# Moving an attention kernel's transposes and softmax sums from TensorE to DMA transposes: linear-memory attention followed by a bilinear feed-forward, one core

## The chip, the cores and the metric

The kernel runs on one core of a Trainium2 chip. A core has TensorE (PE, with its weight loads PEld), VectorE (DVE), ScalarE (ACT), GpSimd (POOL) and SyncE (SP), which work side by side, each on its own queue of instructions in the order in which the program gives them. PE writes to PSUM, which has 8 banks; the other engines read PSUM and SBUF; DMA engines move data between HBM and SBUF, and within SBUF. The metric is the device time of one execution in microseconds, the median over several runs.

## The reference

For each of 8 batches and 8 heads, 576 tokens of head size 64 are attended to through 32 memory slots. phi gives softmax weights over the tokens for each slot; with them the means k_m and v_m of k and v are formed, and each token attends to the 32 means. The result, 4608 tokens of 8 x 64 = 512 values, goes through (x w_a) * (x w_b) w_out with 1536 inner columns.

```python
a = exp(phi - max);  a = a / sum over tokens
k_m = einsum('bhsm,bhsd->bhmd', a, k)
v_m = einsum('bhsm,bhsd->bhmd', a, v)
attn = softmax(q @ k_m.T / 8)          # over the 32 slots
x = attn @ v_m                         # 4608 x 512 after the heads are put side by side
out = ((x @ w_a) * (x @ w_b)) @ w_out
```

## The kernel before

All heads of a batch are handled together. 128 partitions hold 4 heads of 32 slots, so two groups g of 4 heads j make up the 8. Six things are made for a batch: the exponentials of phi (`exp_phi`, ACT); the sums of k, v and of the weights (`kv_sums`, L205, 72 matmuls into two PSUM banks pkv); the means, scaled and laid out twice over (`take_kv`, L221, DVE, tile rep); their transposes kvT (`kv_transpose`, L235, six 128x128 TensorE transposes into pT and one DVE copy); the scores (`scores`, L278, 32 matmuls of 32 rows and 288 columns into four banks pscore) and their exponentials E (`exp_scores`, L301, ACT); and the softmax: denominators by a matmul with a block of ones (`denominators`, L308, four matmuls pD, and logarithms L on ACT) and the product with exp(-L) (`normalise`, L318, ACT and POOL), which gives A. q is transposed on DVE in 32x32 blocks of pairs (`q_transpose`, L200, four a batch, tile qT).

The values are not formed at all: `fold` (L328) multiplies the transposed means of v with w_a and w_b (tiles vab, 48 matmuls a batch, copied out of the banks pva by ACT and DVE in `take_fold`), and the up matmuls pa and pb then multiply A by those. `up_half` (L591) makes 288 tokens of one 128-column block: two matmuls pa, copied out by ACT (a_sb), two matmuls pb, multiplied with a_sb by DVE into ht. The down products take two blocks of 128 tokens together, with 7 products in the place of 8 (`two_downs`, L457, banks py, pv and px, 42 matmuls of 256 columns); POOL adds up their operands h_sums (L448), four sums of 1.64 us for each pair of blocks, and the finished blocks o_sb go out on SyncE's queue (L455).

The order is written out by hand. A batch is a period of 24 steps (`half_steps`), each with the up matmuls of one 288-token half. After each step `work.advance` issues down products at an even rate (`work.plan`), and then the step's slot is run. The slots of the period of batch b prepare batch b+1, and a name with a prime is a unit of batch b+2. The strings `second` (the period of batch 2), `every` (batches 3 to 5) and `last` (batch 6) say which unit stands in which slot (L693 to L695): exp, kv, km, kvt, qt, sc, e, den, nr, v and x are the parts named above, L loads the inputs of the batch after (phi, k, v and q, on POOL's queue), and dN, unused before, issues N down products at once. `work.settle` (L567) issues the down products that are left while a third bank is held for them. Buffers of the pool `mid` and of the inputs are double.

PSUM banks are handed out in turn by `Banks`; a matmul into a bank waits until the engine that reads its old content is done. a_sb has four buffers.

Of the kernel before, what the change touches and what calls it, by code (L numbers as in the profile page):

```python
# [18 lines left out]
def kernel(  # L19
# [26 lines left out]
    mid = ctx.enter_context(tc.tile_pool(name="mid", bufs=2))  # L46
    small = ctx.enter_context(tc.tile_pool(name="small", bufs=2))
# [25 lines left out]
    phis, qs, kvs = {}, {}, {}  # L73
# [71 lines left out]
    banks = Banks()  # L145
# [7 lines left out]
    ident = consts.tile([P, P], F16, name="ident")  # L153
# [23 lines left out]

    attn = {}
    vabs = {}

    def head(g, j):

        jj = j ^ g
        return jj % 2, 2 * g + jj // 2

    def units(b):

        u = {}
        t = {}
# [10 lines left out]
        def q_transpose(hp):  # L200
            if hp == 0:
                t["qT"] = mid.tile([P, NHP, NI * D], F16, name="qT")
            nc.vector.transpose(out=t["qT"][:, hp, :].bitcast(F32), in_=qs[b][:, hp, :].bitcast(F32))  # L203

        def kv_sums():  # L205

            t["pkv"] = [banks.take([P, 3, D], F32, "pkv", hold=True) for _ in range(2)]
            for i in range(NI):
                for g in range(2):
                    for j in range(4):  # L210
                        r, hp = head(g, j)
                        nc.tensor.matmul(  # L212
                            t["pkv"][g][0][32 * j:32 * j + 32],
                            t["exp"][64 * r:64 * r + 64, hp, i, :],
                            kvs[b][64 * r:64 * r + 64, :, hp, D * i:D * (i + 1)],
                            start=(i == 0),
                            stop=(i == NI - 1),
                            tile_position=(64 * r, 32 * j),
                        )

        def take_kv():  # L221

            t["rep"] = mid.tile([P, 2, 3, P], F16, name="rep")
            t["rphi"] = small.tile([P, 2], F32, name="rphi")
            for g in range(2):
                pkv, bank = t["pkv"][g]
                nc.vector.reciprocal(out=t["rphi"][:, g:g + 1], in_=pkv[:, 2, 0:1])
                km = pkv[:, 0].rearrange("p (d e) -> p e d", e=2).unsqueeze(2).to_broadcast([P, 2, 4, 32])
                vm = pkv[:, 1].unsqueeze(1).to_broadcast([P, 2, D])
                for out, x in ((t["rep"][:, g, 0:2].rearrange("p e (z d) -> p e z d", z=4), km),  # L230
                               (t["rep"][:, g, 2].rearrange("p (z d) -> p z d", z=2), vm)):
                    nc.vector.tensor_scalar(out=out, in0=x, scalar1=t["rphi"][:, g:g + 1], scalar2=None, op0=ALU.mult)
                banks.free(bank)

        def kv_transpose():  # L235

            t["kvT"] = mid.tile([P, 6, P], F16, name="kvT")
            pT = banks.tile([P, 6, P], F16, name="pT")
            for g in range(2):
                for x in range(3):  # L240
                    nc.tensor.transpose(out=pT[:, (2 * g + x, 4 + g)[x == 2], :], in_=t["rep"][:, g, x], identity=ident)  # L241
# [36 lines left out]
        def scores(gs):  # L278
# [7 lines left out]
            for dh in range(2):  # L286
                for z in range(2):
                    for g in gs:
                        for j in range(4):
# [8 lines left out]
                                tile_position=(row, 32 * j),  # L298
                            )

        def exp_scores(g):  # L301
# [16 lines left out]
        def normalise(g, hfs=slice(0, 2)):  # L318
# [6 lines left out]
            engine = nc.vector if b < 2 else nc.gpsimd  # L325
            engine.tensor_tensor(out=attn[b][:, g, sl], in0=t["E"][:, g, sl], in1=t["R", g][:, sl], op=ALU.mult)  # L326

        def fold(lo, hi, zs):  # L328
            if b not in vabs:
                vabs[b] = [mid.tile([P, 2, d_ff], F16, name=f"vab{x}") for x in range(2)]  # L330
            if len(zs) > 1 and b > 2:
                work.settle()
            for z in zs:
                t["pva", lo, z] = [banks.take([P, 512], F32, "pva", hold=True) for _ in range(2)]
                for j in range(4):
                    for g in range(2):
                        r, hp = head(g, j)
                        nc.tensor.matmul(  # L338
                            t["pva", lo, z][g][0][32 * j:32 * j + 32, 0:hi - lo],
                            t["kvT"][64 * r:64 * r + 64, 4 + g, M * j:M * j + M],  # L340
                            w_sbs[z][64 * r:64 * r + 64, hp, lo:hi],
                            start=True,
                            stop=True,
                            tile_position=(64 * r, 32 * j),
                        )
# [7 lines left out]
        def one(f, *a):  # L353
            return lambda: f(*a)

        for z in range(2):
            u[f"exp{z}"] = one(exp_phi, z)
            u[f"ks{z}"] = one(sums, z, 0)
            u[f"kt{z}"] = one(transpose, z, 0)
            u[f"vs{z}"] = one(sums, z, 1)  # L360
            u[f"vt{z}"] = one(transpose, z, 1)
            u[f"s{z}"] = one(scores, (z,))
            u[f"e{z}"] = one(exp_scores, z)
# [15 lines left out]
        u["sc"] = one(scores, (0, 1))  # L379
        u["kv"] = one(kv_sums)  # L380
        u["km"] = one(take_kv)
        u["kvt"] = one(kv_transpose)
        u["-"] = lambda: None
        return u

# [200 lines left out]
    work = Work()  # L586
# [147 lines left out]
```

The softmax here doesn't subtract the row's maximum and nothing guards it: scores larger than these inputs give would overflow.

## Time and profile before

| | |
|---|---|
| median of 7 runs | 243.34 us (243.11 to 243.6) |
| the profiled execution | 243.38 us |
| its span, first to last instruction | 241.7 us |
| mean granted TensorE clock | 0.996 |
| busy PE / DVE / ACT / POOL | 231.3 / 167.3 / 157.2 / 159.4 us |
| up matmuls pa and pb, 768 of 288 columns | 75.9 + 74.9 us |
| kvT transposes from rep, 36 | 3.0 us |
| scores, 256 | 5.6 us |
| denominators pD, 32 | 6.7 us |
| DMA, 34.12 MB | mean 141 GB/s |

One execution is profiled on the chip. A group of instructions is listed by line, engine, operation and tile with its count, busy time and mean; since matmuls overlap, the mean of one (0.29 us for 288 columns) is longer than the distance from one start to the next (0.12 us). The first 45 us are filled by the loading of inputs and weights; then batches follow one another every 24 to 25 us from about 78 us on, and the down products of the last tokens end at 238 us. The input loads of batches 4 to 7 are issued by POOL at 72.3, 92.6, 121.9 and 151.8 us.

### The profile page before, as it was taken

What the parts mean: (1) busy time and instruction counts of PE and PEld (TensorE: products, weight loads), DVE (VectorE), ACT (ScalarE), POOL (GpSimd) and SP (SyncE); (2) the same over time, 40 slices, a digit from 0 to 9 for tenths busy, and PEclk for the clock granted to TensorE, in tenths of its full rate; (3) what the DMA queues carried; (4) which work ended last, traced back from release to release, by engine and by line L of the source; (5) the groups of instructions that cost most, each with busy time, mean ns of one, the idle gap of its engine ahead of it and who ended that gap; (6) DMA issues with size and microseconds to landing.
All of it is one profiled execution on the core that took longest, in us unless ns stands there. A gap on an engine that the chain in (4) does not pass through costs nothing.

```text
span 241.7 us, 7803 instructions
## 1 busy us (share of the span) xinstructions
PE 231.3 (96%) x3110; PEld 170.0 (70%) x3110; DVE 167.3 (69%) x406; ACT 157.2 (65%) x410; POOL 159.4 (66%) x135
## 2 busy tenths in 40 slices
PE   7868999999999999999999999999999999999993
PEld 7544664446757867777788777777787778888882
DVE  4736784469858869976984759865986586756652
ACT  2266671569697599598756777587856777465430
POOL 7953244599979549973989759882939087946001
PEclk9999999999999999999999999999999999999998
DMA  6999999999958934992279542794220303032154
GB/s 235 234 197 207 206 258 205 255 208 285 219 130 187 223 75 93 248 185 46 50 171 213 138 90 61 182 207 119 49 46 17 72 17 74 11 81 65 44 127 114
DMA packets 25764, 34.12 MB, mean 141 GB/s; under 512 B 2016, under 2 KB 19808, under 8 KB 25728
## 3 DMA queue, kind: packets, MB, share of 16 engines
q0 software_dynamic: 19264, 23.14, 51.5%
q1 hardware_dynamic: 5952, 9.70, 15.9%
q10 hardware_dynamic: 512, 0.79, 1.0%
q8 instruction: 24, 0.39, 0.6%
q14 instruction: 12, 0.10, 0.1%
HBM read 42.47 MB, written 9.44 MB: 215 GB/s over the span
## 4 chain that ended last, share of the span: by engine, by line
PE 75%; DMA 16%; ACT 2%; POOL 2%; DVE 2%; issue 1%; DVEq 0%; POOLq 0%
PE pa L594 17%; PE py L466 17%; PE pb L594 16%; PE pv L466 9%; DMA wo_sb<-in_moe_w_out_dram 6%; DMA kv_sb<-in_v_dram 5%; DMA wb_sb<-in_moe_w_b_dram 5%; PE pva L338 4%; PE px L466 4%; PE pkv L212 2%; PE po L391 2%; PE pD L315 1%; PE pscore L292 1%; PE pT L241 1%; DVE ht L605 1%
## 5 line engine op out<-in xcount | busy, mean ns | idle before, releaser
L605 DVE TENSOR_TENSOR ht<-a_sb,pb 128x288 f16<-128x288 f16 x168 | 73.3, 448 | 36.3 <-ACT a_sb L602 26.9
L594 PEld LDWEIGHTS <-vab 128*128 128x128 f16 x768 | 71.6, 98 | 27.2 <-issue 9.2
L602 ACT CAST a_sb<-pa 128x288 f16<-128x288 f32 x168 | 66.9, 408 | 26.3 <-PE pa L594 24.8
L594 PE MATMUL pa<-A,vab 128*128 128x288 f16 x384 | 75.9, 287 | 0.2
L594 PE MATMUL pb<-A,vab 128*128 128x288 f16 x384 | 74.9, 286 | 1.0 <-ACT vab L350 0.5
L448 POOL TENSOR_TENSOR h_sums<-ht 128x768 f16<-128x768 f16 x28 | 45.9, 1640 | 32.5 <-DVE ht L605 32.5
L466 PEld LDWEIGHTS <-h_sums 128*128 128x128 f16 x384 | 37.3, 98 | 7.0 <-issue 0.5
L350 DVE CAST vab<-pva 128x512 f16<-128x512 f32 (+1 forms) x52 | 32.5, 644 | 4.6 <-PE pva L338 4.2
L350 ACT CAST vab<-pva 128x512 f16<-128x512 f32 (+1 forms) x52 | 28.1, 570 | 9.4 <-PE pva L338 9.3
L466 PEld LDWEIGHTS <-ht 128*128 128x128 f16 x288 | 28.1, 98 | 5.7 <-issue 0.4
L466 PE MATMUL py<-w_sums,h_sums 128*128 128x256 f16 x192 | 30.4, 272 | 0.0
L448 POOL TENSOR_TENSOR h_sums<-ht,h_sums 128x768 f16<-128x768 f16 x14 | 23.0, 1643 | 0.9
L448 POOL TENSOR_TENSOR h_sums<-h_sums,ht 128x768 f16<-128x768 f16 x14 | 22.9, 1638 | 0.9
L326 POOL TENSOR_TENSOR A<-E,R 128x576 f16<-128x576 f16 x12 | 15.3, 1276 | 7.5 <-ACT R L324 7.2
L305 ACT ACTIVATE E<-pscore 128x288 f16<-128x288 f32 x32 | 11.4, 418 | 11.9 <-PE pscore L292 11.8
L466 PE MATMUL pv<-w_sums,h_sums 128*128 128x256 f16 x96 | 16.2, 273 | 0.0
L466 PE MATMUL py<-wo_sb,ht 128*128 128x256 f16 x96 | 16.0, 273 | 0.0
L473 ACT ACTIVATE u<-py 128x256 f32<-128x256 f32 x32 | 12.5, 391 | 5.0 <-PE py L466 4.8
L466 PE MATMUL py<-w_sums,ht 128*128 128x256 f16 x96 | 15.5, 272 | 0.1
L466 PE MATMUL px<-wo_sb,ht 128*128 128x256 f16 x96 | 15.4, 273 | 0.0
L316 ACT ACTIVATE L<-pD 128x288 f32<-128x288 f32 x32 | 11.6, 427 | 5.1 <-PE pD L315 4.9
L203 DVE STREAM_TRANSPOSE qT<-q_sb 128x288 f32<-128x288 f32 x32 | 14.4, 463 | 0.1
(65 smaller groups left out, 277.6 us busy)
## 6 DMA issues: line engine op xcount, KB each, us to landing
out_dram<-o_sb SPq DMA_DIRECT2D x68, 128.0 KB, 3.0
phi_sb<-in_phi_dram POOLq DMA_DIRECT2D x8, 576.0 KB, 6.2
kv_sb<-in_v_dram POOLq DMA_DIRECT2D x7, 576.0 KB, 10.6
kv_sb<-in_k_dram POOLq DMA_DIRECT2D x7, 576.0 KB, 8.6
q_sb<-in_q_dram POOLq DMA_DIRECT2D x6, 576.0 KB, 13.5
wo_sb<-in_moe_w_out_dram POOLq DMA_DIRECT2D x6, 256.0 KB, 13.7
q_sb<-in_q_dram POOLq DMA_DIRECT2D x4, 288.0 KB, 9.7
wa_sb<-in_moe_w_a_dram POOLq DMA_DIRECT2D x2, 512.0 KB, 13.6
```

What stands on the lines that cost most here:

```text
L203: nc.vector.transpose(out=t["qT"][:, hp, :].bitcast(F32), in_=qs[b][:, hp, :].bitcast(F32))
L305: nc.scalar.activation(out=Ev[:, g, :, z, :], in_=pss, func=AF.Exp, scale=1.0 / (8.0 * CS))
L316: nc.scalar.activation(out=t["L", g][:, sl], in_=pD, func=AF.Ln)
L326: engine.tensor_tensor(out=attn[b][:, g, sl], in0=t["E"][:, g, sl], in1=t["R", g][:, sl], op=ALU.mult)
L338: nc.tensor.matmul(t["pva", lo, z][g][0][32 * j:32 * j + 32, 0:hi - lo], t["kvT"][64 * r:64 * r + 64, 4 + g, M * j:M * j + M], w_sbs[z][64 ...
L350: engine_copy(out=vabs[b][z][:, g, lo:hi], in_=pva[:, 0:hi - lo])
L448: engine.tensor_tensor(out=out, in0=in0, in1=in1, op=op)
L466: nc.tensor.matmul(po, lhs[:, i], rhs[:, i], start=first and i == 0, stop=i == KH - 1, skip_group_check=not first)
L473: nc.scalar.mul(out=x, in_=po, mul=scale)
L594: nc.tensor.matmul(ps, vabs[b][x][:, g, P * i:P * (i + 1)], attn[b][:, g, HALF * hf:HALF * (hf + 1)], start=(g == 0), stop=(g == 1))
L602: nc.scalar.copy(out=a_sbs[b, i, hf], in_=ps)
L605: nc.vector.tensor_tensor(out=ht[:, i, t0:t0 + HALF], in0=a_sbs.pop((b, i, hf)), in1=ps, op=ALU.mult)
```

## The change

For batches from `TURNED = 3` on, three things are turned by DMA transposes on SyncE's queue: q (`q_turn`, 128 x 2304), the means of k and v (`kv_turn`, four blocks of 128x128), which `take_kv` now lays out for k and v in one scaling for each group, and, for batches 4 to 7, the exponentials. The scores then contract over 64 rows in one pass instead of over 32 in two (`token_scores`). For batches 4 to 7 the exponentials E are turned so that tokens lie on partitions (`e_turn`, 128 x 1152); DVE sums the 32 slots of each head (`token_sums`), POOL and DVE multiply with the reciprocals (`token_normalise`), and a second DMA transpose turns the result back (`a_turn`). Batch 3 keeps the denominators by matmul. The slots are placed anew, with down products issued by name (dN). Batches 0 to 2 and the work before the period of batch 2 are as they were.

```diff
+    TURNED = 3
...
+        def q_turn():
+            t["qT"] = mid.tile([P, NHP, NI * D], F16, name="qT")
+            nc.sync.dma_start_transpose(out=t["qT"].rearrange("p c f -> p (c f)").rearrange("p (n x) -> p n x", x=P),
+                                        in_=qs[b].rearrange("p c f -> p (c f)"))
...
-        def take_kv():
+        def take_kv(gs=range(2)):
...
-            for g in range(2):
+            for g in gs:
                 pkv, bank = t["pkv"][g]
                 nc.vector.reciprocal(out=t["rphi"][:, g:g + 1], in_=pkv[:, 2, 0:1])
...
+                if b >= TURNED:
+                    parts = ((t["rep"][:, 2 * g:2 * g + 2].rearrange("p x (z d) -> p x z d", z=2),
+                              pkv[:, 0:2].unsqueeze(2).to_broadcast([P, 2, 2, D])),)
+                for out, x in parts:
                     nc.vector.tensor_scalar(out=out, in0=x, scalar1=t["rphi"][:, g:g + 1], scalar2=None, op0=ALU.mult)
...
+        def kv_turn():
+
+            t["kvT"] = mid.tile([P, 6, P], F16, name="kvT")
+            n = 4 if b >= TURNED else 6
+            nc.sync.dma_start_transpose(out=t["kvT"][:, 0:n], in_=t["rep"][:, 0:n].rearrange("p x d -> p (x d)"))
...
+        def token_scores():
+            t["E"] = mid.tile([P, 2, S], F16, name="E")
+            work.settle()
+            qTv = t["qT"].rearrange("p c f -> p (c f)").rearrange("p (n x) -> p n x", x=P)
+            for g in range(2):
+                t["pss", g] = [banks.take([P, 5 - y, 64], F32, "pscore", hold=True) for y in range(2)]
+            for g in range(2):
+                for x in range(2):
+                    for j in range(4):
+                        r, hp = head(g, j)
+                        y = (hp + x) % 2
+                        n = (NI * hp + y) // 2
+                        nc.tensor.matmul(
+                            t["pss", g][y][0][32 * j:32 * j + 32],
+                            t["kvT"][64 * x:64 * x + 64, 2 * g, M * j:M * j + M],
+                            qTv[64 * x:64 * x + 64, n:n + 5 - y, 64 * r:64 * r + 64],
+                            start=True,
+                            stop=True,
+                            tile_position=(64 * x, 32 * j),
+                        )
...
+        def e_turn():
+            t["ET"] = mid.tile([P, 2, S], F16, name="E").rearrange("p g s -> p (g s)").rearrange("p (n x) -> p n x", x=P)
+            nc.sync.dma_start_transpose(out=t["ET"], in_=t["E"].rearrange("p g s -> p (g s)"))
+
+        def blocks(x):
+            return t["ET"][:, slice(0, 5) if x == 0 else slice(5, 9)].rearrange("p n (j m) -> p (n j) m", m=M)
+
+        def token_sums(x):
+            if x == 0:
+                t["sum"] = small.tile([P, 36], F32, name="sum")
+            out = t["sum"][:, slice(0, 20) if x == 0 else slice(20, 36)]
+            nc.vector.tensor_reduce(out=out, in_=blocks(x), axis=mybir.AxisListType.X, op=ALU.add)
+            nc.vector.reciprocal(out=out, in_=out)
+
+        def token_normalise(x):
+            sums = t["sum"][:, slice(0, 20) if x == 0 else slice(20, 36)]
+            engine = (nc.gpsimd, nc.vector)[x]
+            engine.tensor_tensor(out=blocks(x), in0=blocks(x), in1=sums.unsqueeze(2).to_broadcast(list(blocks(x).shape)),
+                                 op=ALU.mult)
+
+        def a_turn():
+            attn[b] = mid.tile([P, 2, S], F16, name="A")
+            nc.sync.dma_start_transpose(out=attn[b].rearrange("p g s -> p (g s)").rearrange("p (n x) -> p n x", x=P),
+                                        in_=t["ET"].rearrange("p n x -> p (n x)"))
...
-    second = "v2_+x2a_+exp0 x2b_ exp1 - kv+km qt0 kvt+qt1 - qt2+qt3 sc+e0 e1+v0+x0a+x0b den0 nr0+v1+x1a - x1b+exp0' L exp1' v2+x2a den1+qt0'+qt1' x2b - qt2'+nr1+kv'+km' - - kvt'+qt3'"
-    every = "- sc+e0 e1 den0 v0+x0a+x0b - - nr0+exp0' - - v1+x1a qt0' x1b+den1 exp1' - v2+x2a+x2b nr1+qt1' kv'+km' qt2' - qt3' - kvt'+L -"
-    last = "sc+e0 - e1 - v0+x0b - x0a den1 - - den0 v1+x1b x1a+nr0 - - - - nr1+v2+x2a - - - - - x2b"
+    second = "v2_+d1+exp0+x2a_ exp1+d6+x2b_ qd+kv+km0+km1+kvd - - d4 - - sc+e0 - e1+d3+v0+d2+x0a+x0b den0 - v1+nr0+x1a x1b+qd' L+exp0'+d5 - v2+x2a exp1'+x2b - - kv'+den1+nr1+km' kvd' - d7"
+    every = "sc+e0+e1+d3+ed+d3 - - v0+x0a+x0b - sm0 sm1 - tn1+exp0' d5+tn0+exp1' ad v1+x1b+x1a+kv'+km0' qd'+km1' kvd' - - v2+x2b - - - - - L+x2a"
+    last = "sc+e0+e1+ed - - v0+x0b+d5 - - sm0+d4 tn0 sm1+d5 tn1 x0a+v1+x1a+x1b - ad - - v2+x2a - - - d4 - x2b"
```

The new units' names: qd, kvd, ed and ad are the four DMA transposes, km0 and km1 the scaling of one group, sm0 and sm1 the row sums, tn0 (POOL) and tn1 (DVE) the products. `token_exp_scores` reads the four banks pscore as `exp_scores` did, with 320 or 256 columns each.

More of the change, by code (lines that the diff above doesn't have):

```diff
@@ L219, in kv_sums @@
                         )
-        def take_kv():
-            t["rep"] = mid.tile([P, 2, 3, P], F16, name="rep")
-            t["rphi"] = small.tile([P, 2], F32, name="rphi")
-            for g in range(2):
+        def take_kv(gs=range(2)):
+            if gs[0] == 0:
+                t["rep"] = mid.tile([P, 6, P], F16, name="rep")
+                t["rphi"] = small.tile([P, 2], F32, name="rphi")
+            for g in gs:
                 pkv, bank = t["pkv"][g]
@@ L229, in take_kv @@
                 vm = pkv[:, 1].unsqueeze(1).to_broadcast([P, 2, D])
-                for out, x in ((t["rep"][:, g, 0:2].rearrange("p e (z d) -> p e z d", z=4), km),
-                               (t["rep"][:, g, 2].rearrange("p (z d) -> p z d", z=2), vm)):
+                parts = ((t["rep"][:, 2 * g:2 * g + 2].rearrange("p e (z d) -> p e z d", z=4), km),
+                         (t["rep"][:, 4 + g].rearrange("p (z d) -> p z d", z=2), vm))
+                if b >= TURNED:
+                    parts = ((t["rep"][:, 2 * g:2 * g + 2].rearrange("p x (z d) -> p x z d", z=2),
+                              pkv[:, 0:2].unsqueeze(2).to_broadcast([P, 2, 2, D])),)
+                for out, x in parts:
                     nc.vector.tensor_scalar(out=out, in0=x, scalar1=t["rphi"][:, g:g + 1], scalar2=None, op0=ALU.mult)
@@ L238, in kv_transpose @@
             pT = banks.tile([P, 6, P], F16, name="pT")
-            for g in range(2):
-                for x in range(3):
-                    nc.tensor.transpose(out=pT[:, (2 * g + x, 4 + g)[x == 2], :], in_=t["rep"][:, g, x], identity=ident)
+            for x in range(6):
+                nc.tensor.transpose(out=pT[:, x, :], in_=t["rep"][:, x], identity=ident)
             nc.vector.tensor_copy(out=t["kvT"], in_=pT)
+        def kv_turn():
+            t["kvT"] = mid.tile([P, 6, P], F16, name="kvT")
+            n = 4 if b >= TURNED else 6
+            nc.sync.dma_start_transpose(out=t["kvT"][:, 0:n], in_=t["rep"][:, 0:n].rearrange("p x d -> p (x d)"))
         def sums(g, x):
@@ L299, in scores, with token_exp_scores @@
                             )
+        def token_scores():
[18 more added lines that the diff above has]
+                        )
+        def token_exp_scores(g):
+            Ev = t["E"].rearrange("p g (i s) -> p g i s", s=64)
+            for y in range(2):
+                pss, bank = t["pss", g][y]
+                nc.scalar.activation(out=Ev[:, g, y::2, :], in_=pss, func=AF.Exp, scale=1.0 / (8.0 * CS))
+                banks.free(bank)
         def exp_scores(g):
@@ L339, in fold @@
                             t["pva", lo, z][g][0][32 * j:32 * j + 32, 0:hi - lo],
-                            t["kvT"][64 * r:64 * r + 64, 4 + g, M * j:M * j + M],
+                            t["kvT"][64 * r:64 * r + 64, 2 * g + 1 if b >= TURNED else 4 + g, M * j:M * j + M],
                             w_sbs[z][64 * r:64 * r + 64, hp, lo:hi],
@@ L362, in units @@
             u[f"s{z}"] = one(scores, (z,))
-            u[f"e{z}"] = one(exp_scores, z)
+            u[f"e{z}"] = one(token_exp_scores if b >= TURNED else exp_scores, z)
+            u[f"km{z}"] = one(take_kv, (z,))
             u[f"den{z}"] = one(denominators, z)
@@ L378, in units @@
             u[f"qt{x}"] = one(q_transpose, x)
-        u["sc"] = one(scores, (0, 1))
+        u["sc"] = token_scores if b >= TURNED else one(scores, (0, 1))
+        u["qd"] = q_turn
+        u["ed"] = e_turn
+        for x in range(2):
+            u[f"sm{x}"] = one(token_sums, x)
+            u[f"tn{x}"] = one(token_normalise, x)
+        u["ad"] = a_turn
         u["kv"] = one(kv_sums)
@@ L382, in units @@
         u["kvt"] = one(kv_transpose)
+        u["kvd"] = one(kv_turn)
         u["-"] = lambda: None
```

## The prediction

> **What bounds the kernel.** I read the page's busy times first, then the busy times by stretch, because the start, the steady part and the tail have different limits.
>
> ```profile
> PE 231.3 (96%) x3110; PEld 170.0 (70%) x3110; DVE 167.3 (69%) x406; ACT 157.2 (65%) x410; POOL 159.4 (66%) x135
> ...
> 102.00:203.00 101.00, 101.00 (x1306) 77.62 (x1285) 74.14 (x175) 74.37 (x197) 72.98 (x52) 1.00 0.51 105
> 203.00:238.00 35.00, 34.39 (x299) 28.90 (x296) 21.93 (x51) 16.61 (x44) 14.32 (x11) 1.00 0.29 64
> ```
>
> In the stretch lines the columns after the time and its length are busy PE, PEld, DVE, ACT and POOL, then PE clock, DMA share and GB/s. From 102 to 203 us TensorE is busy for 101.00 of 101 us at full clock, while no other compute engine passes 75 us. The waits of PE in that part are short "issue" gaps of its weight loads. So a microsecond of matmul taken out there is a microsecond off the end, and a microsecond for which PE waits is one on it. Between 70 and 102 us it is 31.80 of 32.
>
> Then the timeline of one batch, for what the matmuls concerned really cost. Columns: start, duration, engine, line, operation. Durations overlap in the pipeline, so I take start to start.
>
> ```profile
> 153.72 0.50 PE L241 MATMUL pT<-ident,rep 128*128 128x128 f16 x6
> ...
> 154.05 0.41 PE L594 MATMUL pa<-A,vab 128*128 128x288 f16 x2
> ...
> 156.71 0.47 PE L292 MATMUL pscore<-qT,kvT 32*32 32x288 f16 x32
> ...
> 157.11 0.42 PE L594 MATMUL pa<-A,vab 128*128 128x288 f16 x2
> ...
> 158.87 0.41 PE L315 MATMUL pD<-E,ones 128*128 128x288 f16 x2
> ...
> 159.11 0.41 PE L594 MATMUL pa<-A,vab 128*128 128x288 f16 x2
> ...
> 160.13 0.41 PE L338 MATMUL pva<-wa_sb,kvT 64*32 64x512 f16 x8
> 160.36 0.40 PE L338 MATMUL pva<-wb_sb,kvT 64*32 64x512 f16 x8
> ...
> 160.69 0.36 PEld L594 LDWEIGHTS <-vab 128*128 128x128 f16 x4 [0.42 <-issue]
> ```
>
> Six transposes 0.33 us, 32 score matmuls 0.40, two denominators 0.24, sixteen folds 0.56.
>
> Last the DMA view, in a stretch without an input load (first line) and in one where a load of a batch fills the engines (the other two).
>
> ```profile
> out_dram<-o_sb SPq DMA_DIRECT2D x6, 128.0 KB, 2.4
> ...
> DMA  0684905999899999999999999999999999999400
> ...
> out_dram<-o_sb SPq DMA_DIRECT2D x4, 128.0 KB, 6.0
> ```
>
> The same 128 KB store on SyncE's queue lands 2.4 us after its issue between 108 and 121 us, and 6.0 us after it between 122 and 137 us, while a batch's phi, k, v and q come in (that load takes some 14 us). The new transposes go on this queue.
>
> **What the Trainium skill says.** "VectorE: DVE Perf Modes", section "The three transpose paths", gives 390 ns on TensorE and 1309 ns by DMA for one 128x128 block. TensorE's six cost 0.33 us here, 55 ns each in a row, so its figures are of single ones. "Advanced Engine Details and Errata", "X-Bar Transpose (TRN2)", says such DMAs are as fast as plain ones; no run here shows one. "DMA: Bandwidth & Descriptors", "Issuing engines are not separate DMA queues", says that all issuing engines share the same 16 DMA engines: the 2.4 against 6.0 us agrees. The first page also has `tensor_reduce` at one element a cycle only ("Rules for kernel authors").
>
> **The change, part by part.**
> *PE.* Batches 3 to 7 lose six transposes each: 5 x 0.33 = 1.65 us. Batches 4 to 7 lose four denominators each: 8 pairs x 0.24 = 1.92. The 32 score matmuls of 32 rows become 16 of 64 rows with 320 or 256 columns. The nearest row is the fold (16 of 64 rows, 512 columns, 0.56): 0.56 x 288/512 = 0.31, bounds 0.20 (half of 0.40) and 0.40. Gain 5 x 0.09 = 0.45 (0 to 1.0). Sum 4.0 us. Down products and up matmuls are only moved.
> *ACT*, per turned softmax: four logarithms (0.427) and two exponentials (0.709) go, 3.1 us. *POOL*: two of 1.28 go, one of 640 columns with an fp32 operand comes (1.28 x 640/576 = 1.4, up to double). *DVE*, per batch: four transposes (0.463), one copy (0.551), four scalings (two 0.483, two 0.341) go, 4.05 us; two scalings (0.97) come, with turned softmax two row sums of 640 and 512 elements (0.75 and 0.6, from the 0.684 of a 512-column cast), two reciprocals (0.16 or a little more), one product (0.6): 3.2. All three have a quarter of their time free, so I book nothing for them.
> *DMA.* 18 transposes: q 576 KB (batches 3 to 7), kv 128 KB (the same), E and A 288 KB each (batches 4 to 7). Their cost is only what waits for them. The smallest I give a kv turn is a store's 2.4 us, E 3 to 4; in a load the store's 3.6 us extra comes on top at most, since the turn doesn't write to HBM I take half of it: kv 4.3, E 5.5.
>
> SyncE's queue is in order, but a q turn stands behind only stores, so it starts when its load has landed: for batch 3 at about 70 us, in the gap before the load of batch 4 (issued at 72.3 to 75.3). It is needed at 83. Later ones have over 8 us. Hidden. The A turns are issued some 11 us before their batch begins. Hidden. Three are not clearly hidden; I count PE work in the new order with the durations above, up matmuls at 0.12, down at 0.11.
>
> 1. *Means of batch 3.* Sums end at about 76.7, scaling takes 1.3, turn 4.3 in the load of batch 4: 82.3. PE reaches the scores at 83.5 (84.3 before, less transposes and moved work). Free; with 6 to 6.7 us it is 0.5 to 1.2 late. I book 0.3.
> 2. *Means of batch 4.* Sums are now at the end of the period of batch 2, the turn one slot before the scores. PE has 2 denominators, 12 up and 17 down matmuls between: 0.24 + 1.46 + 1.86 = 3.6 us. Needed: scaling with its place behind one product, 1.5, plus the turn, in the load of batch 5 (issued about 93): 4.3. Late by 2.2 us (0.3 with 2.4, 3.9 with 6). In it lies the second wait there: the last denominators of batch 3 moved behind these sums, and two logarithms, an exponential and POOL's product (2 x 0.43 + 0.71 + 1.28 + one copy 0.41 = 3.3) face 2.6 us of PE work before A of batch 3 is read. Queued behind: everything of PE.
> 3. *E of batches 4 to 7.* The row sums stand in DVE's queue; behind them the products ht, and for those PE's banks and ACT's four a_sb buffers. DVE arrives there 4 to 5 us after E is issued (four exponentials x 0.42, then three products, two folds' copies, two more products), and PE has about 3 us of banks after that. The loads of batches 6 and 7 are issued a few us before E of batches 5 and 6. 5.5 us is covered; I book 0.3 in all.
>
> Sum: -4.0 + 0.3 + 2.2 + 0.3 = -1.2. The profiled execution took 243.38 us, its span 241.7 and 1.7 around it; the median is 243.34, the same within 0.04. 243.34 - 1.2 = **242.1 us**.
>
> **Rivals.**
> *Slower: turns in a load take as long as stores or longer.* For it: 6.0 us in the DMA view, 5.8 to 6.7 from 74 to 90 us, at less than half of E's bytes; the cover of point 2 is short in any case. Against it: the turn writes SBUF. Priced: 1.0 at the scores of batch 3, 3.9 at those of batch 4, and E at 9 us leaves 9 - 4.5 - 3 = 1.5 for each of batches 5 and 6: 7.9 - 4.0 = +3.9, 247.2. It decides from a kv turn of 5.5 us, where point 2 costs 1.5 + 5.5 - 3.6 = 3.4 and the other two bring the sum to the 4.0 gained.
> *Slow in themselves.* 1.31 us a block in a row: E 11.8, kv 5.2, q 23.6 us. Batch 3 waits 70 + 23.6 - 83.5 = 10 us, batch 4 3.1, each E 4.3: +26, 269. Against it: the other page's "as fast as plain".
> *All hidden.* A turn lands like a free store: only 0.3 of point 2 is left, 239.6.
> *The gain is just eaten*, within 0.2%: a kv turn of about 5.3 us.
>
> **Numbers.** 0.2% (0.5 us) is about what a measurement of this kernel can tell. Likeliest, mostly hidden, 240.2 to 242.8: 0.35. All hidden, 239.2 to 240.2: 0.13. Eaten: 0.12. Late in loads, 243.9 to 249: 0.31. Slow turns, 250 to 270: 0.09. So faster 0.48, same 0.12, slower 0.40. The likeliest two have 239.2 to 242.8 for themselves. Below 239.5 lie about 0.05, above 248 some 0.14: range 239.5 to 248.
>
> **What would show it.** The rows of pT<-ident,rep and pD fall from 36 to 6 and from 32 to 16 matmuls, PE busy by 4 us. The list of DMA issues gives kv, E, A and q turns; about 4.3, 5.5, 4 and 5 us. The score rows of batches 3 and 4 show PE's waits (0.3 and 2.2 us); DVE waits for E under 2 us. Wrong would be: E over 8 us or a wait on kvT over 4 (slower), or q turns of batch 3 issued into the load; PE idle between 102 and 203 us above 1.5 us is a wait that I have not seen.

## The result and the profile after

The changed kernel takes 260.87 us (median of 12 runs, 259.71 to 264.01), the kernel before 243.37 us beside it: a ratio of 1.072, 95% interval 1.070 to 1.0743. It is 17.5 us slower. The forecast was 242.1 us, its range 239.5 to 248, its first choice "faster" (0.48, against 0.40 for slower): wrong in sign and in size. The profiled execution below was the slowest of the twelve, 264.01 us with a span of 262.3, which is why sums over it come out some 3 us above the median, and the ratios in this document leave out runs in a slower state, which the medians include, so that the two can differ a little.

The page's busy times and the row of PE's granted clock:

```profile
PE 234.8 (90%) x2984; PEld 170.0 (65%) x2984; DVE 164.7 (63%) x391; ACT 150.4 (57%) x386; POOL 154.3 (59%) x131
...
PEclk9999999999999689959999999999599999999998
```

PE has 126 matmuls fewer than before and yet 3.5 us more busy time. The clock row says why: it falls to 0.5 or 0.6 in three of the 40 slices, and a matmul at half clock is busy longer (0.66 us where it took 0.41, shown further below). Now the busy times by stretch (the columns are those of the stretch lines in the prediction: time, length, PE, PEld, DVE, ACT, POOL, clock, DMA share, GB/s).

```profile
84.00:88.00 4.00, 0.44 (x16) 0.15 (x16) 0.00 (x0) 0.00 (x0) 0.00 (x0) 0.84 1.17 219
88.00:92.00 4.00, 4.00 (x40) 1.76 (x29) 1.28 (x3) 2.53 (x7) 0.00 (x0) 0.50 0.17 55
...
102.00:203.00 101.00, 87.43 (x1111) 65.94 (x1108) 63.75 (x149) 56.78 (x147) 60.22 (x44) 0.93 0.82 151
```

From 102 to 203 us PE stands still for 13.6 of 101 us, where it never stood before. From 84 to 88 us every compute engine is all but idle while the DMA engines are full; from 88 to 92 the DMA engines are nearly free and PE works at a clock of 0.50. The list of waits names what ended each gap (total, times, longest):

```profile
PE pscore L329 <- DMA kvT<-rep: 10.3, 2, 6.1
...
DVE sum L383 <- DMA E<-E: 7.9, 2, 4.5
...
PE pa L671 <- DVE ht L682: 4.1, 1, 4.1
...
PE py L543 <- DVE o_sb L554: 3.3, 1, 3.3
```

Two waits of PE are for the transposed means themselves (batch 3: 4.2 us, batch 4: 6.1). The other two name DVE, but DVE had been waiting for E of batches 5 and 6. Together PE waits 17.7 us. Its waits name no input load, so no batch came late because its own inputs did. The chain of what ended last has the DMA transposes in it (start, time):

```profile
78.11 9.40 DMA kvT<-rep
...
105.02 8.59 DMA kvT<-rep
...
173.07 8.75 DMA E<-E
```

POOL issues the input loads of batches 4 to 7 at 72.3, 100.2, 132.7 and 164.4 us. Each of these transposes was issued 5 to 9 us after the start of one; so was E of batch 5 (issued at 140.97, 9.1 us). The DMA view of 104 to 116 us shows one transpose in a load and one just after it (the first row is the busy share of the 16 engines in 40 slices, the last number of the others the us from issue to landing):

```profile
DMA  9999999999999999999999999999999999630000
...
kvT<-rep SPq DMA_TRANSPOSE x1, 8.6
E<-E SPq DMA_TRANSPOSE x1, 3.2
```

The means (128 KB), issued at 105.0 in the load, land at 113.6, about 0.6 us before the engines fall free. E of batch 4, more than twice the bytes, is issued at 115.6 and takes 3.2 us. This pair is the case in short: the transposes are not slow in themselves; they are late beside a load.

### The profile page after: what moved, and what is told of

Same layout as the page of the kernel before. It is cut to its first block, busy times and chain, and to the rows that moved or that the text cites. A ratio compares the mean times of both kernels' runs of the same rounds, so it can differ in the third digit from the quotient of the medians.

```text
span 262.3 us, 7547 instructions
## 1 busy us (share of the span) xinstructions
PE 234.8 (90%) x2984; PEld 170.0 (65%) x2984; DVE 164.7 (63%) x391; ACT 150.4 (57%) x386; POOL 154.3 (59%) x131
## 3 DMA queue, kind: packets, MB, share of 16 engines
q1 hardware_dynamic: 29824, 15.67, 29.2%
## 4 chain that ended last, share of the span: by engine, by line
PE 75%; DMA 15%; ACT 4%; DVE 3%; issue 2%; DVEq 0%; SPq 0%; POOLq 0%
PE pa L671 17%; PE pb L671 16%; PE py L543 14%; DMA kvT<-rep 7%; PE pv L543 7%; PE pva L407 5%; PE po L468 4%; PE px L543 3%; DMA E<-E 3%; DMA phi_sb<-in_phi_dram 2%; DMA out_dram<-o_sb 2%; PE pkv L218 2%; PE pk L271 1%; PE pscore L308 1%; PE pscore L329 1%
## 5 line engine op out<-in xcount | busy, mean ns | idle before, releaser
L671 PEld LDWEIGHTS <-vab 128*128 128x128 f16 x768 | 74.0, 100 | 31.5 <-issue 11.3
L671 PE MATMUL pa<-A,vab 128*128 128x288 f16 x384 | 78.0, 293 | 4.2 <-DVE ht L682 4.1
L671 PE MATMUL pb<-A,vab 128*128 128x288 f16 x384 | 77.1, 293 | 1.0 <-ACT vab L419 0.5
L543 PEld LDWEIGHTS <-h_sums 128*128 128x128 f16 x384 | 38.0, 100 | 10.0 <-issue 2.8
L543 PE MATMUL py<-w_sums,h_sums 128*128 128x256 f16 x192 | 32.0, 282 | 0.0
L543 PE MATMUL px<-wo_sb,ht 128*128 128x256 f16 x96 | 16.1, 280 | 0.0
L550 ACT ACTIVATE u<-py 128x256 f32<-128x256 f32 x32 | 12.5, 391 | 5.1 <-PE py L543 4.8
L342 ACT ACTIVATE E<-pscore 128x320 f16<-128x320 f32 (+1 forms) x20 | 6.7, 416 | 14.0 <-PE pscore L329 14.0
L389 POOL TENSOR_TENSOR E<-E,sum 128x640 f16<-128x640 f16 x4 | 5.1, 1263 | 16.1 <-PE py L543 8.9
L543 PE MATMUL pv<-wo_sb,h_sums 128*128 128x256 f16 x96 | 14.1, 277 | 0.0
L195 ACT ACTIVATE exp_sb<-phi_sb 128x576 f16<-128x576 f32 x16 | 10.9, 696 | 5.4 <-DMA phi_sb<-in_phi_dram 5.4
## 6 DMA issues: line engine op xcount, KB each, us to landing
wa_sb<-in_moe_w_a_dram POOLq DMA_DIRECT2D x2, 512.0 KB, 13.6
```

The costliest lines, as they stand in the source:

```text
L195: nc.scalar.activation(out=t["exp"][:, 2 * z:2 * z + 2, :, :], in_=phis[b][:, 2 * z:2 * z + 2, :].rearrange("p c (i m) -> p c i m", m=M), ...
L342: nc.scalar.activation(out=Ev[:, g, y::2, :], in_=pss, func=AF.Exp, scale=1.0 / (8.0 * CS))
L543: nc.tensor.matmul(po, lhs[:, i], rhs[:, i], start=first and i == 0, stop=i == KH - 1, skip_group_check=not first)
L550: nc.scalar.mul(out=x, in_=po, mul=scale)
L671: nc.tensor.matmul(ps, vabs[b][x][:, g, P * i:P * (i + 1)], attn[b][:, g, HALF * hf:HALF * (hf + 1)], start=(g == 0), stop=(g == 1))
```

## The experiments

Three theories are put against each other in the expectations. The first (A): the transposes are quick but land late beside an input load. The second (B): the transposes, or the new order of the slots, cost time with or without loads. The third (C): part of the time is PE's clock after a long wait. The expectations are quoted as they stood before each run.

### No loads beside, in both kernels

```diff
     def load(b):
+        if b >= 4:
+            phis[b], kvs[b], qs[b] = phis[b - 2], kv_sbs[b % 2], qs[b - 2]
+            return
         load_phi(b)
```

> The kernel before, with the input loads of batches 4 to 7 left out (these batches compute on the inputs of batches 2 and 3 that are still in SBUF, so the output of half the batches differs). It is the control of the next run. Both theories: TensorE bounds it, the loads are hidden, 243.3 us, within 0.5.

> The changed kernel with the same loads left out. Theory A (the DMA transposes are quick by themselves and are held up by the input loads on the same DMA engines): kv turns land in 2.4 to 3 us, E turns in 3.2 to 4, no wait of PE over 1 us, and the time is 4.0 us less matmul work plus some 0.5 us: about 240 us. Theory B (the turns, or the new order of the units, are slow in themselves): kv and E turns still near 9 us, waits of PE at the scores of batches 3 and 4 remain, 250 us or more.

Batches 4 to 7 use the inputs of earlier batches here. The kernel before does not care: 243.45 us, ratio 1.0006 (0.9997 to 1.0016). The changed kernel falls from 260.87 to 238.63 us, ratio 0.9805 (0.9788 to 0.9822). Its DMA view:

```profile
qT<-q_sb SPq DMA_TRANSPOSE x5, 4.8
kvT<-rep SPq DMA_TRANSPOSE x5, 2.4
E<-E SPq DMA_TRANSPOSE x4, 3.2
A<-E SPq DMA_TRANSPOSE x4, 3.5
```

and its stretch line, PE full again:

```profile
102.00:203.00 101.00, 101.00 (x1227) 78.76 (x1226) 79.53 (x181) 68.90 (x179) 64.79 (x41) 1.00 0.49 93
```

The second theory falls: with free DMA engines all 18 transposes and the new order of slots gain 4.8 us against the same kernel before. All of the loss, and more, needs a load beside the transposes. That leaving out the loads also spares the waits for inputs does not matter here: PE had none in the changed kernel. This kernel's span of 237.0 us is the base of the sums below.

### Only the means of batches 3 and 4 by TensorE

```diff
             n = 4 if b >= TURNED else 6
+            if b in (3, 4):
+                pT = banks.tile([P, n, P], F16, name="pT")
+                for x in range(n):
+                    nc.tensor.transpose(out=pT[:, x, :], in_=t["rep"][:, x], identity=ident)
+                nc.vector.tensor_copy(out=t["kvT"][:, 0:n], in_=pT)
+                return
             nc.sync.dma_start_transpose(
```

with these units two slots later and one slot later in `second`.

> Only the means of batches 3 and 4 go back to TensorE transposes (two slots later than their DMA turns stood); the rest is the changed kernel. Theory A: PE's two waits for kvT (4.2 and 6.1 us in the profile) and the half clock after each (about 2.4 us each) go, four transposes of 0.055 us come for each: 260.9 - 10.3 - 4.8 + 0.4 = 246 us. If the waits merely move to the next late thing: 255 us or more.

253.79 us (249.45 to 271.08), ratio 1.0455 (1.0406 to 1.0505). Both waits for kvT are gone, but 7 us come back instead of 15. The profiled execution is the quickest of the six, 249.45 us; what the others lose beyond it no trace shows. Without the waits everything is earlier, and so E of batch 4, which in the changed kernel came after the load (3.2 us), is now issued within the load of batch 5:

```profile
102.47 7.76 DMA E<-E
...
161.58 8.30 DMA E<-E
```

```profile
PE pa L677 <- DVE ht L688: 3.7, 1, 3.7
PE pb L677 <- DVE ht L688: 3.3, 1, 3.3
...
PE py L549 <- DVE o_sb L560: 1.7, 1, 1.7
```

A wait removed moved the next transpose into a load: three waits behind E (batches 4, 5 and 6) in the place of two.

### The loads of batches 6 and 7 eight slots earlier

```diff
-    every = "sc+e0+e1+d3+ed+d3 - - v0+x0a+x0b - sm0 sm1 - tn1+exp0' d5+tn0+exp1' ad v1+x1b+x1a+kv'+km0' qd'+km1' kvd' - - v2+x2b - - - - - L+x2a"
+    every = "sc+e0+e1+d3+ed+d3 - - v0+x0a+x0b - sm0 sm1 - tn1+exp0' d5+tn0+exp1' ad v1+x1b+x1a+kv'+km0' qd'+km1' kvd' L - v2+x2b - - - - - x2a"
```

> Only the loads of batches 6 and 7 are moved, from slot 22 to slot 14 of the string every, so that they end before or about when E of the next batch is turned. Theory A: E turns of batches 5 and 6 land in under 6 us, the two waits of PE (3.3 and 4.1 us) and one half-clock stretch (2.4 us) go: 260.9 - 9.8 = 251 us. If the E turns are slow for another reason: 260 to 261 us.

255.72 us, ratio 1.0479 (1.0411 to 1.0548): 5 of the 10 us expected. POOL issued these loads only 3 to 6 us earlier (129.5 and 158.4 us): its queue is not tied to PE's slots. E still takes 6.4 and 7.2 us, not under 6. That is enough to let PE's two waits on E fall from 3.3 and 4.1 to 0.5 and 2.6 us in the profiled execution (258.62 us), since the load beside them ends earlier; the waits on kvT stay (10.6 us).

### The same 128 KB copied, not transposed

```diff
             n = 4 if b >= TURNED else 6
+            if b in (3, 4):
+                nc.sync.dma_start(out=t["kvT"][:, 0:n], in_=t["rep"][:, 0:n])
+                return
             nc.sync.dma_start_transpose(
```

> The turn of the means of batches 3 and 4 becomes a plain DMA copy of the same 128 KB (not transposed, so the values of these batches are wrong), on the same queue at the same place. Queue theory (anything put on this queue in a load waits for the load): still 6 to 9 us to landing, waits of 3 us or more at both scores, 255 to 261 us. Form theory (the transposes' 256-byte packets are what is held up): 3 to 5 us, as little as 0 to 2 us of wait, 247 to 250 us.

The chain of this kernel has both copies:

```profile
93.76 6.37 DMA kvT<-rep
...
114.86 5.60 DMA kvT<-rep
```

A plain copy within SBUF in a load takes 5.6 to 6.4 us, as long as a store does there (6.0 us), so the place of the data is not the point. The transposed form of the same bytes, issued at about the same point of its load (4.8 and 5.9 us after the load's start, the copies 4.3 and 5.9), takes 8.6 to 9.4. With free DMA engines a copy takes 2.0 us (a later run has it) and the transpose 2.4: a load adds 3.6 to 4.4 us to the one and 6.2 to 7.0 to the other, so some 2.6 us of its extra are the form's. Both theories of the expectation have a part. Median 255.62 us, ratio 1.0453 (1.0391 to 1.0516), in the range of the first of the two. PE still waits 4.3 us for the copies. (The profiled execution, 268.08 us, has a wait of 12.9 us at 49 to 62 us, before any of this, behind a single product of DVE that took 13.6 us, as one execution of the kernel of before without loads has it too (12.5 us of wait); it stays out of the sum below.)

### PE kept busy in the two waits

```diff
             work.settle()
+            if b in (3, 4):
+                fill({3: 19, 4: 28}[b])
             qTv = t["qT"].rearrange("p c f -> p (c f)")
```

> The changed kernel, with matmuls of zeros put on PE right ahead of the scores of batches 3 and 4: 19 and 28 of 512 columns, 0.21 us each at full clock, 4.1 and 6.0 us, as long as PE waited there for kvT. Theory C (an idle PE is given half the clock afterwards): the kvT waits are filled, the clock stays at 1.0 there, and what the slow stretches after them cost (two times about 2.4 us) comes back: 256 us. Theory A without C (only the wait itself costs): 261 us, no gain.

260.17 us, ratio 1.0665 (1.0629 to 1.0701): hardly less than the changed kernel. The clock did hold,

```profile
70.00:102.00 32.00, 31.29 (x452) 21.34 (x444) 21.13 (x48) 22.42 (x57) 21.26 (x19) 1.00 0.80 151
```

(and at the second fill too), but the transposes landed later still (9.92 and 10.35 us), so that 2.4 us of waiting were left behind the fills, and the waits on E, now 2.4 and 3.1 us, cost 3.2 us of clock. By its time alone the run speaks against the third theory; with several things moving at once it decided nothing, and the question of the clock was put again without loads.

### Late transposes without a load, bare and filled

```diff
             n = 4 if b >= TURNED else 6
+            if b in (3, 4):
+                for h in range(3):
+                    hop = mid.tile([P, 6, P], F16, name="rep")
+                    nc.sync.dma_start(out=hop[:, 0:n], in_=t["rep"][:, 0:n])
+                    t["rep"] = hop
             nc.sync.dma_start_transpose(
```

The loads of batches 4 to 7 are left out as above. The second of the two has the fills of the last section as well.

> The changed kernel without the input loads of batches 4 to 7 (these batches compute on older inputs), with three plain copies of the 128 KB on SyncE's queue ahead of the DMA transpose of the means of batches 3 and 4: the transposes are late without any load beside them. Copies of 2.4 us and the transpose of 2.4 us make about 10 us from the first issue, against 9.4 and 8.6 us in the loads. PE then waits about 4.8 us at the scores of batch 3 and 7.5 us at those of batch 4, 12.3 us in all. Theory 'waits alone': 238.6 + 12.3 = 250.9 us. Theory 'waits and half clock after them' (5 us at half clock after each, 2.5 us lost twice): 255.5 us, and PE's clock under 0.6 for some 5 us after both waits.

> As the kernel with the late transposes and no loads, with 19 and 28 matmuls of zeros (128x512, 0.22 us each, results not used) on PE ahead of the scores of batches 3 and 4, so that PE has work in most of the two waits (4.1 and 6.1 us of it). Theory 'half clock after waits': the clock stays at 1.00 and the time falls by some 4 us against the kernel without the fill, to about 251 us. Theory 'waits alone': the same time as without the fill, 0.3 us either way.

The bare kernel takes 251.26 us (250.56 to 251.81), ratio 1.0324 (1.0306 to 1.0343). A copy took 2.0 us and not 2.4, so the waits are shorter than expected:

```profile
PE pscore L337 <- DMA kvT<-rep: 9.3, 2, 5.9
```

238.63 + 9.3 = 247.9; 3.3 us more were measured. The stretches in which PE works after its two waits:

```profile
88.00:92.00 4.00, 4.00 (x35) 2.07 (x34) 2.34 (x5) 2.83 (x8) 0.00 (x0) 0.65 0.32 73
...
112.00:116.00 4.00, 4.00 (x36) 2.60 (x28) 1.39 (x4) 2.52 (x7) 0.00 (x0) 0.66 0.38 74
```

Summed over stretches of 1 us, PE's busy time times one minus its clock is 3.3 us in this execution: the missing 3.3 us. The filled kernel takes 250.47 us (250.37 to 250.93), with a clock of 1.00 throughout in its profiled execution: 238.63 + 10.4 of fill (19 take 4.19 us) + 1.4 of waiting = 250.4. It is 0.8 us quicker, not 4 and not the same, because fills and rest of the wait were 2.5 us longer than the waits that they replaced (3.3 - 2.5 = 0.8); that the clock holds, and that the sum closes without a clock term when it does, is what the third theory says. So these waits cost their own length and then the clock.

### The loads set apart from the transposes

The means of batches 3 and 4 by TensorE again; the q transpose of batch 4 and the load of batch 5 earlier; and in `every` the load in two parts, k and v (La) after E is expected to land, phi and q (Lb) after the transposes of q and the means:

```diff
-    second = "v2_+d1+exp0+x2a_ exp1+d6+x2b_ qd+kv+km0+km1+kvd - - d4 - - sc+e0 - e1+d3+v0+d2+x0a+x0b den0 - v1+nr0+x1a x1b+qd' L+exp0'+d5 - v2+x2a exp1'+x2b - - kv'+den1+nr1+km' kvd' - d7"
-    every = "sc+e0+e1+d3+ed+d3 - - v0+x0a+x0b - sm0 sm1 - tn1+exp0' d5+tn0+exp1' ad v1+x1b+x1a+kv'+km0' qd'+km1' kvd' - - v2+x2b - - - - - L+x2a"
+    second = "v2_+d1+exp0+x2a_ exp1+d6+x2b_ qd+kv+km0+km1 - kvd d4 - - sc+e0 qd' e1+d3+v0+d2+x0a+x0b den0 L v1+nr0+x1a x1b exp0'+d5 - v2+x2a exp1'+x2b - - kv'+den1+nr1+km' - kvd' d7"
+    every = "sc+e0+e1+d3+ed+d3 - - v0+x0a+x0b - sm0 sm1+La - tn1+exp0' d5+tn0+exp1' ad v1+x1b+x1a+kv'+km0' qd'+km1' kvd' - - v2+x2b+Lb - - - - - x2a"
```

> A version that keeps turns and loads apart: means of batches 3 and 4 by TensorE, q of batch 4 turned and batch 5 loaded some slots earlier, and the loads of batches 6 and 7 in two parts, k and v in slot 6 (when E has landed) and phi and q in slot 16 (when kv has). Theory A: no E turn over 5 us, the kernel without loads plus 0.4 us of transposes, 239 to 240.5 us, 0.985 of the kernel before. If loads and turns can't be kept apart: 243 us or more.

243.62 us (20 runs, 241.71 to 257.84), ratio 0.9969 (0.9946 to 0.9991): some 17 us of the changed kernel's loss are gone with all loads in place, but not the 239 to 240.5 us expected. One late transpose is left, E of batch 4 in the load of batch 5 (issued at 91 us):

```profile
102.40 7.46 DMA E<-E
```

```profile
PE pb L677 <- DVE ht L688: 3.0, 1, 3.0
```

Four more runs tried to free this one too.

> As the kernel with the loads set apart, but k and v of the batch after are issued by POOL behind the product that waits for E, so that they cannot start before E has landed. The transpose of E of batch 4 then shares its time with the last 4 us of the load of batch 5 only: about 4.5 us in the place of 7.46, and PE's wait of 3.0 us falls to about 0.3. Theory 'transposes late in loads': 243.6 - 2.7 = 240.9 us. Rival 'the load comes late in turn' (k and v some 5 us later, sums of the next batch wait): 243 to 246 us.

In `every`, La moved from slot 6 to slot 9, behind the product on POOL. 259.67 us, ratio 1.0627 (1.0581 to 1.0673), far outside both expectations. E of batch 4 came down to 4.8 us, but k and v, issued at 110.5 us, and phi and q at 117.8 now met the transposes of A, q and the means of batch 5, all three. The DMA view of 108 to 140 us:

```profile
A<-E SPq DMA_TRANSPOSE x1, 10.6
qT<-q_sb SPq DMA_TRANSPOSE x1, 23.2
kvT<-rep SPq DMA_TRANSPOSE x1, 13.0
```

```profile
PE pscore L335 <- DMA kvT<-rep: 15.4, 2, 12.9
```

SyncE itself was held for 10.6 us at issuing the q transpose, and the transpose of the means stood behind it. Instead of one wait of 3 us there are one of 12.9 and one of 2.6.

> As the kernel with POOL's loads behind E, and the load of batch 5 six slots earlier (issued at about 83 in the place of 91 us), so that it has ended when E of batch 4 is issued at 102. All E transposes about 3.2 to 4 us, no PE wait above 1 us from 78 us on. Theory 'transposes late in loads': 238.6 (no loads at all) plus 0.5 for what loads still do, 239.2 us. Rival: the load of batch 5 stands on that of batch 4 and delays q of batch 4 or its phi: PE waits of 2 us or more before 104 us, 242 us or more.

The same with the load of batch 5 at slot 6 of `second`: 263.26 us, ratio 1.0796 (1.0756 to 1.0837). E now takes 3.2 us, as expected, but the means of batch 5 take 17.5 us (wait 15.7), and q of batch 4 costs 2.1.

> As the kernel with the loads set apart (k and v of the later batches stay at slot 6), with the load of batch 5 three slots earlier, directly behind the q transpose of batch 4: issued at about 87 in the place of 91 us, ended at about 101.5, just ahead of E of batch 4 at 102.4. Theory 'a transpose lands when the load beside it ends': E of batch 4 takes about 4 us in the place of 7.46, PE's wait of 3.0 us goes, 243.6 - 2.7 = 240.9 us. Rival 'the q transpose of batch 4 takes its place': q, issued at 89, lands after 102 and the scores of batch 4 wait 1 to 2 us: 243 us or more.

> The same with the load of batch 5 five slots earlier, issued at about 84 us, right behind the end of the load of batch 4. E of batch 4 is free of it by 3 us: 3.2 us. The q transpose of batch 4, issued at 89 with 12 us of the load beside it, takes 12 us or more and the scores of batch 4 at 102 wait for it by up to 2 us, as in the kernel with the load at 82 us (2.1 us): 242 us. Theory without such a limit: 240.9 us as with three slots.

These two left La at slot 6 and moved only the load of batch 5, in `second` from slot 12 to slot 9 or 7. They take 242.99 us, ratio 0.9976 (0.9967 to 0.9984), and 243.48 us, ratio 1.0004 (0.9986 to 1.0022). The load went out at 81.9 and 82.8 us, not at 87 and 84: POOL takes its next instruction when its own inputs are there. The rival was right, q took E's place:

```profile
PE pscore L335 <- DMA qT<-q_sb: 2.4, 1, 2.4
PE pscore L335 <- DMA kvT<-rep: 1.6, 2, 1.2
```

With the load at slot 9 the wait on E is gone, 2.4 us are spent waiting for q and 1.6 for means. It has the lowest median with real inputs, 0.4 us below the kernel of before (243.39 beside it) and 4.4 us above the kernel without loads. By the ratios it (0.9976) and the first version (0.9969) are 0.2 to 0.3% below the kernel of before; neither is clearly the better one, and both differ from it by next to nothing.

### The sum that closes

Each profiled span against 237.0 us, the span without loads. "Clock" is PE's busy time times one minus its clock, summed over stretches of 1 us from 60 to 245 us; "work" is what the edit adds on PE (0.22 us a fill matmul; 0.4 us for eight transposes).

| kernel | this execution (median) | span | PE's waits from 60 us on | clock | work | 237.0 + sum |
|---|---|---|---|---|---|---|
| changed | 264.0 (260.9) | 262.3 | 17.7 | 7.8 | 0 | 262.5 |
| means 3, 4 by TensorE | 249.5 (253.8) | 247.8 | 8.7 | 1.5 | 0.4 | 247.6 |
| loads earlier | 258.6 (255.7) | 256.9 | 13.7 | 5.9 | 0 | 256.6 |
| waits filled | 260.2 (260.2) | 258.5 | 7.9 | 3.2 | 10.3 | 258.4 |
| late, no loads | 251.2 (251.3) | 249.4 | 9.3 | 3.3 | 0 | 249.6 |
| late, no loads, filled | 250.4 (250.5) | 248.7 | 1.4 | 0 | 10.4 | 248.8 |
| loads apart | 243.6 (243.6) | 241.9 | 3.0 | 1.7 | 0.4 | 242.1 |
| loads apart, load of 5 at slot 9 | 243.0 (243.0) | 241.3 | 4.0 | 0 | 0.4 | 241.4 |

All of these close within 0.3 us, each for its one execution. Of those not in the table, La at slot 9 and the load of batch 5 at slot 7 miss by 0.6 and 0.7 us: their executions reach the batches later (the load of batch 4 goes out at 73.0 and 73.1 us, not at 72.2). The changed kernel is thus its kernel without loads, plus four waits on late transposes, plus the clock that these waits cost.

## Why the prediction was wrong, step by step

**PE's work: right, 0.8 us too small.** The sum gave -4.0 us; with no transpose late, -4.8 were measured. The row of 16 score matmuls took 0.40 us and not 0.31, so that term (0.45 us) was nothing; what makes up the other 1.2 us was not found out. That DVE, ACT and POOL stay covered held: with free DMA engines PE is busy for 101.00 of 101 us. So did "Hidden" for the q and A transposes of the changed kernel. (DVE's row sums were put at 0.75 and 0.6 us from a cast of 512 columns in 0.684; that cast gives 0.86 and 0.68, and 0.82 and 0.68 were measured. It decided nothing.)

**Points 1 and 2, the means: the step that failed is the time of a transpose in a load.** I took the free 2.4 us (right to the digit) and half of a store's extra 3.6, "since the turn doesn't write to HBM": 4.3. (Half of 3.6 on 2.4 is 4.2; the 0.1 doesn't matter.) Measured were 9.40 and 8.59. The plain copy, which does not write to HBM either, pays 3.6 to 4.4 on its free 2.0 us, so halving was the first error; taking the store's extra as an upper end for a transpose, which paid 6.2 to 7.0, was the second, and larger. Waits of 0.3 and 2.2 us became 4.2 and 6.1. The rest of the two points held: the means of batch 3 were issued at 78.1 us (78.0 forecast) and PE reached the scores at 83.4 (83.5); with 9.4 and 8.6 us the prediction's own sums give 3.9 and 6.5. In the total, 2.8 us of waits were booked; 17.7 were measured, and 7.8 of clock on top.

**Point 3, E: the same error, and a missed piece of work.** Booked 5.5 us, measured 9.1 and 8.7 in loads. The rival "Slower" priced E at 9 us with 1.5 us of waiting each; 3.3 and 4.1 were measured. DVE's timeline of batch 5 has most of the difference:

```profile
150.10 0.82 DVE L383 TENSOR_REDUCE sum<-E 128x20 f32<-128x640 f16 x1 [3.41 <-DMA E<-E]
150.95 0.28 DVE L384 RECIPROCAL sum<-sum 128x20 f32<-128x20 f32 x1
...
152.98 0.41 DVE L554 SCALAR_TENSOR_TENSOR o_sb<-py,u 128x256 f32<-128x256 f32 x1
```

After E has landed, 1.1 us of sums and reciprocals stand ahead of the first product that gives PE a bank; in batch 6 that is what PE waits for, and it goes on 1.5 us after the landing. In batch 5 PE's next matmul needs the bank py, which DVE reads only at 152.98, behind both row sums, so PE goes on at 153.45, 3.4 us after the landing. I counted when DVE arrives at the sums and how long PE's banks last after that, but not how long DVE needs from E's landing to the bank that PE needs. In batch 5 a store of o_sb issued at 145.2 also landed only at 151.2. It does not seem to have cost anything: DVE is busy without a gap from 150.1 on, and its next product follows the reciprocals after 0.20 us, as in batch 6 (0.19), where no such store is late.

**The clock: a term that was not in the sum.** No wait in the kernel of before is long, so its profile has nothing on what follows one. The Trainium skill has it: "TensorE: Matmul & The Clock Gate", "Part 1: The HAM clock gate", says that after an idle window of about 3.4 us PE's clock is halved, until it has been busy for about as long, and that the window runs freely. The trace agrees for the long waits. After the waits of 4.2, 6.1 and 4.1 us the stretches show 0.50, and PE's timeline shows matmuls of 0.66 us that elsewhere take 0.41:

```profile
87.56 0.74 PE L329 MATMUL pscore<-qT,kvT 64*32 64x320 f16 x16 [4.18 <-DMA kvT<-rep]
88.23 0.66 PE L671 MATMUL pa<-A,vab 128*128 128x288 f16 x2
```

The limit is lower and not sharp here. In the traces of this case, from 60 us on, all eleven waits of PE of 3.9 us or more were followed by half clock, and none of 2.1 us or less. Of those between 2.4 and 3.7 us eight were and six were not: 3.3 us in the changed kernel and 3.7 us with the means by TensorE cost no clock, while 2.4 us in the kernel with filled waits did, some 2.1 us after the wait began:

```profile
PE py L545 <- DVE o_sb L556: 2.4, 1, 2.4
...
149.00:150.00 1.00, 0.00 (x0) 0.00 (x0) 0.97 (x4) 0.00 (x0) 1.00 (x2) 1.00 0.00 0
150.00:151.00 1.00, 0.62 (x4) 0.42 (x4) 1.00 (x5) 0.00 (x0) 0.97 (x1) 0.53 0.00 0
```

So an idle time shorter than the page's 3.4 us can do it, and the measurement decides. I should have looked it up for the rival: from some 2.4 us on a wait can cost, and from 3.9 us on it did each time, its length and 1.5 to 3 us more (3.3 us for two waits without loads, 7.8 for three in the profiled execution of the changed kernel).

**The rivals.** "Slower: turns in a load take as long as stores or longer" named place and mechanism, and its point of decision, a turn of 5.5 us, was passed. Its 9 us for E was right; its 247.2 us was too small in the rest: 9 us and not 6 for the means, waits on E more than twice as long, no clock. "Slow in themselves" (269 us) has the time nearest to the measured one, by luck, for its mechanism is wrong: free transposes take 2.4 and 3.2 us. The signs that I gave for "wrong" all came: E over 8 us, waits on kvT over 4, PE idle above 1.5 us.

**The skill's other page.** "Advanced Engine Details and Errata", "X-Bar Transpose (TRN2)", calls such DMAs as fast as plain ones. For a free queue the runs agree (2.4 us, as a store). Beside a load they do not (8.6 to 9.4 against 5.6 to 6.4 for the plain copy), and the measurement decides. I cited the sentence as a point against the slow rivals without asking under which load it holds.

**Open.** Why a transpose loses more than a plain copy to a load was not shown. One candidate is the size of its packets: with the transposes the packets of SyncE's queue rise from 5,952 to 29,824 for 6 MB more, some 250 bytes each, and each plain copy of the means needed 400 packets fewer than the transpose in its place. But form and packet size changed together there, and no run parts them. Nor is it shown why waits of the same length cost clock in one place and not in another.

## What to carry to other kernels

A DMA moved onto a dependency chain must be priced in the stretch in which it will be issued: here 128 KB transposed took 2.4 us on free engines and about 9 beside an input load, and every slot won elsewhere may carry the next one into a load. Price a wait with what follows it, the work that stands between the arrival and the first release, and PE's clock if the wait passes some 2.4 us (here it cost from 3.9 us on always, below that in places). And to separate "slow" from "late", take the other traffic away in one run: it gave the whole answer at once, 260.9 against 238.6 us.

## What was not expected of the hardware

- A plain SBUF copy of 128 KB took 2.0 us free and 5.6 to 6.4 beside a load; a transpose 2.4 and 8.6 to 9.4. With a batch's load and three transposes together, a q transpose of 576 KB took 23.2 us (free 4.8), and SyncE needed 10.6 us to issue it (free 2.8 to 3.7).
- POOL's place in the order of slots says little on when its loads go out: moved eight slots they went 3 to 6 us earlier, moved three slots 9 us.
- Waits of PE of 2.4, 2.6 and 3.0 us were followed by half clock, others of 3.3 and 3.7 us were not.
